# A gated linear attention with an MLP: the order of the twelve sequence pairs and the rings of the states

## The chip, the cores and the metric

The kernel runs on one core of one Trainium2 chip. Its time is the device time in microseconds (us), the median of several runs. A core has five engines that matter here: PE (matrix products), DVE and ACT (elementwise work; both can read the accumulators), POOL (elementwise work in on-chip memory only) and SP (here it issues DMAs).

## The reference

Cut to what matters, for 4 batches, 8 heads, 768 steps and a head size of 48:

```python
mag = np.sqrt(a_re * a_re + a_im * a_im)
scale = np.minimum(mag, 0.999) / (mag + 1e-06)
a_re_n, a_im_n = (a_re * scale, a_im * scale)
for t in range(S):
    S_re, S_im = ar * S_re - ai * S_im + kv[t], ar * S_im + ai * S_re
    y[t] = q[t] @ S_re
x = y, with heads side by side                # (4, 768, 384)
xn = (x - mean) / sqrt(var + 1e-6) * g_ln
out = x + relu(xn @ w_ch1) @ w_ch2            # 384 -> 1536 -> 384
```

A complex state per head is turned and shrunk at each step by a complex gate, and gains the outer product of k and v. The output of each step goes through a layer norm and an MLP with a residual.

## The kernel before, in words

Each batch is a sequence of 768 steps. It is cut into 6 chunks of 128 steps, and two chunks make a pair: 3 pairs per sequence, 12 pairs `P` in all, 24 chunks `n`. Within a chunk the recurrence is written as a small masked attention: magnitudes and phases of the gates are summed along time, keys and queries are scaled by them, and the state is carried from chunk to chunk.

For one pair the steps are these, by the names of the order table:

- `are`, `aim`, `k`, `q`, `vf`: loads, issued by SP (L400, L448, L452).
- `ln`, `iv`, `r`, `r2`, `u`, `l`, `lc`, `th`: the gates' log magnitude and angle (L455 to L492).
- `dec` on PE (L484) sums log magnitudes; `e` and `en` (L488) are its exponentials. `ph` on PE (L499, L503) sums angles, starting from the carry `car` that the pair before it in the same sequence has left (L513, L516); `sin`, `abs` or `qt`, `cos` follow.
- `ke`, `qe`, then `ks`, `qs` (all recorded at L292): keys and queries times magnitude, then times cosine and sine. Index 0 and 1 at the end are two halves.
- For each chunk: `kT`, `qT` on PE (L598) and `ksT`, `qsT` turn them, or a DMA does; `am` (L621) is the product, `atm` (L292) its masked copy; `gm` (L645) is the new part of the state and `G` the state; `gs` is a sum on the way to it, `dps` and `decc` bring the decay of a whole pair; `y` (L682, L685) is the output of the chunk.
- `bn`, `x`, `xr`, `xtr`, `xT`, `rstd`: layer norm and the turned input of the MLP.
- `mm1` (L752, six groups of six products per pair), `relu` (L764 on ACT, L766 on DVE), `mm2` (L776, three groups of four per chunk), `oa` and `ot` (scale and residual), `st` (the store).

The MLP weights come by two DMAs from POOL's queue, `wl.0` into `w1b` (L365) and `wl.1` into `w2b` (L367). `wc.J.E` (L381) then scales a block of w1b by the layer norm's gain. Before w1b is there, PE also runs `warm` products (L806, L810) whose results nobody reads.

Nothing decides the order at run time. A table `PLAN` lists every step with its engine and its accumulator bank, and each engine runs its own steps in the order of the table:

```python
vf.0.1:S th.0.0:A r2.0.0:V warm.w0:P0 ... wl.0:G@qs.0.0.0 qT.0:P2 q.2.1:S v.0:V
```

The letter is the engine (P, A, V, G for POOL, S), the digit behind it the bank. `@qs.0.0.0` makes a step on POOL wait for that DVE step too. Tiles live in rings of a fixed number of buffers (`RINGS`); a step that writes slot `i` waits until all users of `i` minus the ring's length are done. Pairs are numbered sequence by sequence (`b, pp = divmod(P, PB)`): pairs 0, 1, 2 are sequence 0, pairs 3, 4, 5 sequence 1, and so on. So the state `G` and the carry `car` pass from a pair to the next number, and rings of four and two hold them. Pair 0 is worked in two halves of the heads (`PARTS`).

Of the kernel before, what the change touches and what calls it, by code (L numbers as in the profile page):

```python
# [52 lines left out]
warm.10:P4 dec.1.0:P4 en.0.0:A7 uthc:V vf.0.0:S e.0.0:A7 r.2.0:V e.1.0:A4 warm.11:P1 warm.12:P1 dps.0:P7 are.3.0:S
r2.2.0:V en.1.0:A4 ke.0.0.0:V u.2.0:A gln:S ke.0.1.0:V qe.0.0.0:V aim.3.0:S qe.1.0.1:V qe.1.0.0:V k.1.0:S l.2.0:V
tab.trig.3:A sin.0.0:A6 sin.0.1:A0 warm.w30:P1 warm.w31:P1 warm.w32:P1 warm.w33:P1 warm.13:P1 warm.14:P1@en.1.0
warm.w34:P1 warm.w35:P1 warm.w36:P1 warm.w37:P1 warm.15:P1 warm.16:P1@qe.0.0.0 warm.w38:P1 warm.w39:P1 warm.w40:P1
warm.17:P1 warm.18:P1 warm.19:P1 warm.20:P1 qt.0.0:P6 qs.0.0.1:V sin.1.0:A2 qt.0.1:P0 ks.0.0.1:V vf.1.1:S lc.2.0:V
cos.0.0:A6 ks.0.1.1:V warm.21:P1 warm.22:P1 qt.1.0:P2 qs.1.0.1:V cos.0.1:A0 vf.1.0:S dps.1:P5 qs.0.1.1:V cos.1.0:A2
dec.2.0:P0 ks.0.1.0:V k.2.1:S ks.0.0.0:V decc.0:A7 qs.0.1.0:V kT.0:P6 decc.1:A5 qs.0.0.0:V th.2.0:A qs.1.0.0:V
wl.0:G@qs.0.0.0 qT.0:P2 q.2.1:S v.0:V qT.1:P3 ksT.0:A6 qsT.0:V2 qT.2:P4 ke.1.0.0:G@v.0 k.2.0:S kT.1:P5 qsT.1:A3  # L60
qsT.2:V4 am.0:P6 ke.1.0.1:G@v.0 ksT.1:V5 gm.0:P4 atm.0:V6 ks.1.0.1:G warm.23:P2 warm.24:P2 am.1:P2 qT.3:P5 tab.log.4:A
ln.3.0:A atm.1:V2 y.0:P6 ks.1.0.0:G G.0:A4 e.2.0:A0 warm.w41:P7 warm.25:P7 warm.26:P7 warm.27:P7 gm.1:P4 bn.0:V6
ph.2.0:P2 iv.3.0:A qsT.3:V5 one:G kT.2:P7 x.0:A6 G.1:V4 r.3.0:G en.2.0:A0 ksT.2:V7 warm.28:P5 xtr.0:P6 kT.3:P4 xT.0:V6
am.2:P0 ksT.3:V4 y.1:P5 v.1:G atm.2:V0 am.3:P6 tab.trig.5:A th.3.0:A xr.0:G gm.2:P4 bn.1:V5 ngl:G sin.2.0:A2 r2.3.0:G
ph.3.0:P0 atm.3:V6 x.1:A5 q.2.0:S car.3.0:A0 y.2:P5 G.2:V4 sin.3.0:A0 xtr.1:P7 qt.2.0:P2 are.4.0:S wc.1.1:V gm.3:P4
xT.1:A7 wc.1.0:V qt.3.0:P0 wc.1.2:V cos.2.0:A2 wl.1:G@xT.1 vf.2.0:S wc.0.0:V mm1.0.1.0:P6 wc.0.1:V cos.3.0:A0 bn.2:V5
y.3:P3 aim.4.0:S mm1.0.1.1:P6 wc.0.2:V x.2:A5 wc.2.1:V wc.2.2:V mm1.0.0.1:P0 wc.2.0:V relu.0.1:A6 bn.3:V3
qe.2.0.1:G@wc.2.0 xtr.2:P2 mm1.0.0.0:P0 xT.2:V2 x.3:V3 ke.2.0.1:G@wc.2.0 mm1.0.2.1:P6 gs.3:V4 xtr.3:P2 mm1.0.2.0:P6
rstd.1:G xT.3:V2 tab.log.6:A u.3.0:A ke.2.0.0:V mm1.1.0.1:P2 relu.0.0:A0 l.3.0:V mm1.1.1.0:P4 relu.0.2:A6 mm1.1.1.1:P4
ks.2.0.0:V lc.3.0:V mm1.1.2.1:P0 ks.2.0.1:V relu.1.1:A4 qe.2.0.0:V dec.3.0:P6 rstd.0:A qs.2.0.0:V mm1.1.0.0:P2  # L70
en.3.0:A6 qs.2.0.1:V kT.5:P4 vf.2.1:S e.3.0:A6 qT.4:P5 mm1.1.2.0:P0 ksT.5:A4 qsT.4:V5 qT.5:P6 are.5.0:S G.3:V
relu.1.2:A0 kT.4:P5 qsT.5:V6 mm2.0.0:P4 are.6.0:S ksT.4:V5 ln.4.0:A am.5:P6 mm2.0.1:P4 iv.4.0:A atm.5:V6 aim.5.0:S
mm2.0.2:P4 relu.1.0:A2 am.4:P0 r.4.0:V q.3.0:S mm2.1.0:P5 atm.4:V0 r2.4.0:A v.2:G@r.4.0 mm2.1.1:P5 q.3.1:S mm2.1.2:P5
xr.2:G@r.4.0 u.4.0:A ot.0:V4 mm2.2.0:P6 ln.5.0:A l.4.0:V st.0:S gm.4:P2 mm2.2.1:P6 iv.5.0:A G.4:V2 y.4:P0 lc.4.0:V
ln.6.0:A mm2.2.2:P6 xr.3:V k.3.0:S bn.4:V0 xr.1:G@xr.3 dec.4.0:P2 iv.6.0:A r.5.0:G@xr.3 k.3.1:S x.4:V0 y.5:P1 e.4.0:A2
dps.3:P4 bn.5:V1 xtr.4:P0 vf.3.1:S mm2.3.0:P7 oa.2:A6 xT.4:V0 en.4.0:A2 vf.3.0:S x.5:V1 mm2.3.1:P7 qe.3.0.0:G ot.1:V5
r2.5.0:A xtr.5:P0 k.4.1:S mm2.3.2:P7 rstd.2:G xT.5:V0 qe.3.0.1:V mm1.2.0.0:P0 u.5.0:A aim.6.0:S qs.3.0.0:V
mm1.2.0.1:P0 qs.3.0.1:V q.4.1:S mm1.2.2.1:P2 ke.3.0.0:V ot.3:V7 mm1.2.2.0:P2 k.4.0:S tab.trig.7:A th.4.0:A ke.3.0.1:V
qT.6:P5 relu.2.2:A2 ks.3.0.0:V ph.4.0:P6 q.4.0:S decc.3:V4 ks.3.0.1:V relu.2.0:A0 mm1.2.1.0:P2 l.5.0:V k.5.0:S kT.7:P4
abs.4.0:A6 qsT.6:V5 v.3:G@l.5.0 dps.4:P1 car.4.0:A6 kT.6:P0 vf.4.0:S ksT.7:V4 sin.4.0:A6 r.6.0:G@l.5.0 qT.7:P5  # L80
ksT.6:V0 mm1.2.1.1:P2 are.8.0:S decc.4:A1 qsT.7:V5 th.5.0:A am.6:P6 st.1:S gm.6:P4 relu.2.1:A2 ot.2:G ph.5.0:P0
atm.6:V6 are.7.0:S th.6.0:A ke.4.0.0:G am.7:P2 G.6:V4 y.6:P5 sin.5.0:A0 mm2.5.0:P6 atm.7:V2 ke.4.0.1:G vf.4.1:S
cos.4.0:A mm2.5.1:P6 qe.4.0.1:G bn.6:V5 mm2.5.2:P6 abs.5.0:A0 q.5.0:S ks.4.0.1:V y.7:P2 cos.5.0:A q.5.1:S lc.5.0:V
gm.7:P4 mm2.4.0:P7 ks.4.0.0:V x.6:A5 bn.7:V2 mm2.4.1:P7 xr.5:G@ks.4.0.0 r2.6.0:A aim.7.0:S G.7:V4 qe.4.0.0:G@ks.4.0.0
mm2.4.2:P7 x.7:V2 k.7.0:S dec.5.0:P0 qs.4.0.0:V xtr.6:P2 qs.4.0.1:V xtr.7:P3 st.2:S kT.9:P4 tab.log.8:A e.5.0:A0
xT.6:V2 v.4:G@qs.4.0.1 qT.8:P5 xT.7:V3 en.5.0:A0 ksT.9:V4 mm1.3.1.0:P2 ksT.8:S xr.4:V ln.7.0:A qT.9:P4 qsT.8:V5
qe.5.0.0:G@xr.4 mm1.3.1.1:P2 u.6.0:A qsT.9:V4 aim.8.0:S mm1.3.2.0:P0 relu.3.1:A2 l.6.0:V am.9:P4 st.3:S mm1.3.2.1:P0
iv.7.0:A k.5.1:S lc.6.0:V atm.9:V4 mm1.3.0.0:P2 qe.5.0.1:G@lc.6.0 ln.8.0:A mm1.3.0.1:P2 relu.3.2:A0 r.7.0:G@lc.6.0
ot.4:V7 dec.6.0:P4 vf.5.1:S ot.5:V6 relu.3.0:A2 gm.8:P7 ph.6.0:P0 G.8:V7 rstd.3:G vf.6.1:S en.6.0:A4 qs.5.0.1:V
am.8:P2 r2.7.0:V st.4:S e.6.0:A4 mm2.6.0:P6 qs.5.0.0:V iv.8.0:A mm2.6.1:P6 atm.8:V2 k.6.0:S xr.7:G@qs.5.0.0 mm2.6.2:P6  # L90
u.7.0:A xr.6:G@qs.5.0.0 vf.5.0:S abs.6.0:V0 r.8.0:G@qs.5.0.0 y.9:P4 y.8:P2 k.6.1:S bn.9:V4 mm2.7.0:P3 q.7.1:S bn.8:V2
gm.9:P7 tab.trig.9:A sin.6.0:A0 mm2.7.1:P3 ke.5.0.1:G gs.9:V7 are.9.0:S x.9:A4 mm2.7.2:P3 ot.6:V6 ke.5.0.0:G th.7.0:A
qT.11:P4 x.8:V2 st.6:S dps.6:P5 G.9:G cos.6.0:A car.6.0:V0 qT.10:P2 q.6.0:S qsT.11:V4 xtr.8:P6 ke.6.0.0:G xtr.9:P7
ph.7.0:P0 xT.8:A6 xT.9:V7 th.8.0:A qsT.10:V2 q.6.1:S mm1.4.1.1:P6 l.7.0:V decc.6:A5 car.7.0:A0 mm1.4.0.1:P4 abs.7.0:A0
ks.5.0.0:V mm1.4.0.0:P4 r2.8.0:V aim.9.0:S sin.7.0:A0 ks.5.0.1:V mm1.4.1.0:P6 relu.4.0:A4 lc.7.0:V kT.10:P1 ot.7:V3
q.7.0:S ke.6.0.1:G@lc.7.0 kT.11:P2 relu.4.1:A6 ksT.10:V1 k.7.1:S mm1.4.2.0:P4 ksT.11:V2 st.5:S am.10:P0 ks.6.0.1:V
am.11:P6 atm.10:V0 dec.7.0:P2 v.5:G@ks.6.0.1 tab.log.10:A rstd.4:A mm1.4.2.1:P4 ln.9.0:A vf.6.0:S xr.8:G@ks.6.0.1
# [749 lines left out]
```

## Time and profile before

| what | value |
|---|---|
| median of 3 runs | 188.05 us (187.25 to 188.61) |
| the profiled execution | 187.51 us, span 185.6 us |
| PE busy | 177.0 us, 95% of the span |
| DVE, ACT, POOL busy | 157.7, 154.6, 99.8 us |
| DMA issues by SP, share of the 16 DMA engines | 81.4% |
| moved by DMA | 35.34 MB, mean 190 GB/s |

The span runs from the first to the last instruction of the program; the device time has 1.9 us more around it. Busy time of an engine is the time in which at least one of its instructions ran. Products on PE overlap one another, so their mean duration (273 ns for one of mm1) is longer than the distance from one to the next.

### The profile page before, as it was taken

To read this page: it belongs to the slowest core of one execution; us is meant where nothing else is said; L and a number is where in the kernel's file an instruction comes from. 1 tells how busy PE (TensorE), PEld (TensorE's weight loads), DVE (VectorE), ACT (ScalarE), POOL (GpSimd) and SP (SyncE) were. 2 spreads that over 40 slices of the span, in tenths; PEclk is the share of its full clock that TensorE was granted. 3 is DMA by queue.
4 is the path that set the end of the run, shared out by engine and by line. 5 is a ranking of instruction groups with operands and counts; after the bars stand their busy time and mean duration, and the time that the engine had idled before them with its cause. 6 is when DMAs were issued, how large, how long until landed. Compare 5 with 4: busy or idle time off the path is not lost.

```text
span 185.6 us, 5131 instructions
## 1 busy us (share of the span) xinstructions
PE 177.0 (95%) x2029; PEld 139.0 (75%) x2029; DVE 157.7 (85%) x302; ACT 154.6 (83%) x218; POOL 99.8 (54%) x128
## 2 busy tenths in 40 slices
...
GB/s 154 309 229 206 246 199 191 206 143 189 262 187 213 226 228 230 212 273 181 222 238 151 168 150 241 190 227 200 183 159 139 246 147 202 163 193 73 70 82 87
DMA packets 128440, 35.34 MB, mean 190 GB/s; under 512 B 124448, under 2 KB 127648, under 8 KB 128416
## 3 DMA queue, kind: packets, MB, share of 16 engines
q1 hardware_dynamic: 127616, 32.65, 81.4%
...
HBM read 28.31 MB, written 4.72 MB: 178 GB/s over the span
## 4 chain that ended last, share of the span: by engine, by line
PE 59%; ACT 14%; DMA 10%; DVE 10%; issue 3%; SPq 2%; DVEq 0%
PE banks L752 22%; PE banks L776 19%; DMA w1b<-in_moe_w_ch_dram 7%; PE banks L598 4%; PE banks L621 4%; ACT L815 3%; PE banks L484 2%; DMA are<-in_a_re_dram 2%; DMA k<-in_k_dram 2%; ACT are L457 2%; PE banks L682 2%; DVE l L473 1%; ACT h L764 1%; PE banks L685 1%; ACT w L455 1%
## 5 line engine op out<-in xcount | busy, mean ns | idle before, releaser
L752 PE MATMUL banks<-xT,w1b 128*128 128x256 bf16 x432 | 52.7, 273 | 0.2
L776 PE MATMUL banks<-w2b,h 128*128 128x384 bf16 (+2 forms) x300 | 52.5, 319 | 0.0
L752 PEld LDWEIGHTS <-w1b 128*128 128x128 bf16 x432 | 45.8, 114 | 1.7 <-DVE w1b L381 0.4
L764 ACT ACTIVATE h<-banks 128x1024 bf16<-128x1024 f32 x33 | 32.8, 1022 | 8.3 <-PE banks L752 8.1
L776 PEld LDWEIGHTS <-h 128*128 128x128 bf16 x300 | 26.9, 97 | 14.1
L292 DVE TENSOR_TENSOR atm<-banks,mask 128x1024 bf16<-128x1024 f32 x24 | 28.9, 1218 | 1.9 <-PE banks L621 1.6
L815 ACT ACT_TABLE_LOAD x15 | 19.2, 1283 | 1.0 <-PEq L831 0.8
L292 POOL TENSOR_TENSOR ke<-k,en 128x384 bf16<-128x384 f32 x14 | 12.7, 916 | 8.3 <-DVE l L476 5.6
L292 POOL TENSOR_TENSOR qe<-q,e 128x384 bf16<-128x384 f32 x15 | 13.7, 916 | 6.1 <-DVE w1b L381 1.9
L292 POOL TENSOR_TENSOR ks<-ke,trig 128x768 bf16<-128x768 bf16 x7 | 11.4, 1643 | 6.4 <-PE banks L752 4.2
L621 PE MATMUL banks<-qsT,ksT 128*128 128x128 bf16 x192 | 14.6, 219 | 0.1
L410 POOL TENSOR_SCALAR v<-vf 128x768 bf16<-128x768 f32 x7 | 5.8, 831 | 16.0 <-DVE r L292 8.9
L810 PE MATMUL banks<-u_e 128*128 128x512 f16 x42 | 11.7, 418 | 2.2 <-POOL u_e L320 2.2
L292 POOL TENSOR_TENSOR r<-aim,are 128x768 f16<-128x768 f32 x7 | 12.7, 1817 | 1.9 <-ACT x L699 1.5
L709 POOL TENSOR_SCALAR xr<-x,mv 128x384 f32<-128x384 bf16 x16 | 9.3, 586 | 8.1 <-PE banks L752 3.3
L621 PEld LDWEIGHTS <-ksT 128*128 128x128 bf16 x192 | 12.0, 98 | 1.8 <-DVE ksT L289 0.5
L692 DVE BATCH_NORM_STATS2 stats<-banks 128x6 f32<-128x384 f32 x24 | 13.4, 556 | 0.1
L682 PE MATMUL banks<-v,atm 128*128 128x48 bf16 x192 | 12.1, 183 | 0.3 <-ACT x L699 0.2
L473 DVE SCALAR_TENSOR_TENSOR l<-r,w 128x768 f16<-128x768 f16 (+1 forms) x13 | 11.5, 892 | 0.9 <-ACT r L469 0.7
L791 DVE SCALAR_TENSOR_TENSOR ot<-banks,rstd,xr 128x384 f32<-128x384 f32 (+2 forms) x18 | 10.5, 590 | 2.0 <-PE banks L776 1.6
L455 ACT ACTIVATE w<-are 128x768 f32<-128x768 f32 (+1 forms) x13 | 10.2, 790 | 2.3 <-DMA are<-in_a_re_dram 2.3
L682 PEld LDWEIGHTS <-atm 128*128 128x128 bf16 x192 | 11.0, 96 | 1.2 <-DVE atm L292 0.2
...
## 6 DMA issues: line engine op xcount, KB each, us to landing
...
```

The lines of the kernel that those rows point to most:

```text
L292: {"DVE": nc.vector, "POOL": nc.gpsimd}[eng(name)].tensor_tensor(**kw)
L455: add(f"ln.{X}", lambda S_=S_: act(out=S_("w"), in_=S_("are"), func=AF.Ln), needs=[f"are.{X}"], uses=[("are", P), ("w", P)])
L473: nc.vector.scalar_tensor_tensor(out=S_("l"), in0=S_("r2"), scalar=0.5, in1=S_("w"), op0=ALU.mult, op1=ALU.add)
L621: nc.tensor.matmul(ps[:, h], lhsT=T("ksT", n)[:, h], rhs=T("qsT", n)[:, h], start=True, stop=True)
L682: nc.tensor.matmul(ps[:, h], lhsT=T("atm", n)[:, h], rhs=T("v", P)[:, c, h], start=True, stop=nfirst)
L692: nc.vector.bn_stats(out=T("stats", n), in_=bank(f"y.{n}")[:, 0:DM])
L752: nc.tensor.matmul(ps[:, jj], lhsT=w1b[:, dc, ts(gi, JG * C)].rearrange("k (p j) -> k j p", j=JG)[:, jj], rhs=T("xT", P)[:, dc].rearrange( ...
L764: act(out=dst, in_=src, func=AF.Relu)
L776: nc.tensor.matmul(bank(f"o.{N}")[:, ws], lhsT=T("h", P)[:, j, ts(c, C)], rhs=w2b[:, j, ws], start=(j == 0), stop=(j == NJ - 1))
L791: nc.vector.scalar_tensor_tensor(out=o, in0=bank(f"o.{N}")[:, ws], scalar=T("rstd", P)[:, ds(c, 1)], in1=xs, op0=ALU.mult, op1=ALU.add)
L810: g.add(f"warm.w{i}", lambda i=i: nc.tensor.matmul(bank(f"warm.w{i}"), lhsT=u_e[:, 0, 0], rhs=u_e.rearrange("p c j t -> p (c j t)"), start ...
L815: g.add(f"tab.{nm}.{i}", lambda tab=tab: nc.scalar.preload_act_table_set(tab))
```

## The change

Pairs are numbered the other way: first the first pairs of all four sequences (0 to 3), then the middle ones (4 to 7), then the last ones (8 to 11). The pair before pair `P` in its sequence is now `P - 4` and not `P - 1`. The state at the end of a pair therefore lives through four pairs: `G` is kept by pair, in a ring of 5, and the state in the middle of a pair moves to a ring of its own, `Gh`, of 2. The phase carry's ring grows from 2 to 4. All of this changes only which buffer a step names and which step it waits for; every step computes what it did. The order table is a new one throughout: steps stand in another order, some are given to another engine, and two warm-up products are wide that were narrow.

```diff
 RINGS = {...
-         "ks": 3, "qs": 3, "ksT": 4, "qsT": 4, "atm": 3, "G": 4, "x": 10, "stats": 4,
-         "mv": 5, "rstd": 5, "xT": 3, "h": 2, "ot": 3, "car": 2, "gt": 2, "xr": 3}
+         "ks": 3, "qs": 3, "ksT": 4, "qsT": 4, "atm": 3, "G": 5, "Gh": 2, "x": 10, "stats": 4,
+         "mv": 5, "rstd": 5, "xT": 3, "h": 2, "ot": 3, "car": 4, "gt": 2, "xr": 3}
...
 def pair_ops(P):
-    b, pp = divmod(P, PB)
+    pp, b = divmod(P, B)
+    was = P - B
+    back = was * R + R - 1
...
-                + ([] if first else [f"car.{P - 1}.{x}" for x in range(PARTS.get(P - 1, 1))]),
+                + ([] if first else [f"car.{was}.{x}" for x in range(PARTS.get(was, 1))]),
...
-                        act(out=T("car", P + 1)[96:C, fs], ...
+                        act(out=T("car", P + B)[96:C, fs], ...
...
                 elif c == 0:
-                        f"G.{n}", out=T("G", n), ..., in1=T("G", n - 1), op=ALU.add),
-                        needs=[f"gm.{n}", f"G.{n - 1}"], uses=[("G", n), ("G", n - 1)],
+                        f"G.{n}", out=T("Gh", P), ..., in1=T("G", was), op=ALU.add),
+                        needs=[f"gm.{n}", f"G.{back}"], uses=[("Gh", P), ("G", was)],
...
-                        nc.tensor.matmul(ps[:, h], lhsT=T("qsT", n)[:, h], rhs=T("G", n - 1)[:, h],
+                        nc.tensor.matmul(ps[:, h], lhsT=T("qsT", n)[:, h], rhs=(T("Gh", P) if c else T("G", was))[:, h],
...
-for i in range(29):   # warm.i, 256 columns
+for i in range(27):
-for i in range(42):   # warm.wi, 512 columns
+for i in range(44):
```

In the order tables, around the trigger of w1b (before, then after):

```diff
-qs.0.0.1:V ... ks.0.0.1:V ... lc.2.0:V ... ks.0.1.1:V ... qs.1.0.1:V ... qs.0.1.1:V ... ks.0.1.0:V ... ks.0.0.0:V
-... qs.0.1.0:V ... qs.0.0.0:V th.2.0:A qs.1.0.0:V wl.0:G@qs.0.0.0
+lc.2.0:V ... decc.1:V2 ... qs.0.1.1:V ks.0.1.1:V cos.0.0:A3 qs.0.0.1:V warm.17:P1 warm.18:P1 qt.1.0:P6 wl.0:G@qs.0.0.1
```

and around the first mm1:

```diff
-wc.1.1:V gm.3:P4 xT.1:A7 wc.1.0:V qt.3.0:P0 wc.1.2:V cos.2.0:A2 wl.1:G@xT.1 vf.2.0:S wc.0.0:V mm1.0.1.0:P6
+wc.2.2:V warm.25:P1 xtr.0:P0 atm.2:V2 car.3.0:A4 xtr.1:P1 wc.2.1:A ... wc.2.0:A xT.0:V0 are.4.0:S xT.1:V1 gm.2:P2
+cos.3.0:A4 wc.1.2:V y.2:P3 mm1.0.2.1:P0 wc.0.0:V wc.0.1:V wl.1:G@wc.0.0
```

More of the change, by code (lines that the diff above doesn't have):

```diff
@@ L53 @@
[L53 to L97, printed above, removed]
@@ L138 @@
[L138 to L141 removed]
+ue:G are.1.0:S are.0.0:S are.0.1:S pad.qs.1:G car0.0:G aim.1.0:S ident:G pad.ks.0:G mask:G aim.0.0:S tab.log.0:A
+ln.1.0:A pick:G aim.0.1:S iv.1.0:A one:G car0.1:G aim.2.0:S pad.qs.0:G ln.0.0:A car0.3:G ln.0.1:A zdec:G qrow:G
@@ new lines @@
+qs.2.0.0:V tab.log.6:A u.3.0:A ks.2.0.1:V mm1.1.2.1:P4 relu.1.1:A6 qs.2.0.1:V mm1.1.2.0:P4 ks.2.0.0:V relu.0.1:A0
+qT.5:P3 pad.ks.2:G@ks.2.0.0 mm1.1.0.1:P6 xr.0:G@ks.2.0.0 qsT.5:V3 relu.1.2:A4 kT.4:P0 l.3.0:V kT.5:P1 ksT.4:A0
+vf.2.1:S mm1.1.0.0:P6 G.3:V2 lc.3.0:V qT.4:P3 ksT.5:V1 uec:G@lc.3.0 dec.3.0:P4 are.5.0:S ln.4.0:A qsT.4:V3 am.5:P0
+uthc:V rstd.1:A mm2.0.0:P2 atm.5:V0 iv.4.0:A xr.1:G@uthc q.3.1:S mm2.0.1:P2 relu.1.0:A6 mm2.0.2:P2 r.4.0:V q.3.0:S
+e.3.0:A4 am.4:P0 r2.4.0:V mm2.2.0:P3 aim.5.0:S atm.4:V0 u.4.0:A v.2:G@r2.4.0 mm2.2.1:P3 en.3.0:A4 mm2.2.2:P3 rstd.0:G
@@ new lines @@
+l.5.0:V aim.6.0:S kT.7:P4 tab.trig.7:A th.5.0:A decc.3:V7 mm1.2.2.0:P0 ke.4.0.0:G@l.5.0 q.4.1:S ksT.7:V4 relu.2.0:A2
+ph.5.0:P6 relu.2.2:V0 xr.3:G@l.5.0 st.2:S th.4.0:A ke.4.0.1:G kT.6:P4 ot.3:V5 am.7:P2 sin.5.0:A6 are.7.0:S xr.4:G
+ksT.6:V4 ph.4.0:P0 abs.5.0:A6 v.3:G atm.7:V2 mm1.2.1.0:P4 car.5.0:A6 are.8.0:S car.4.0:A0 am.6:P6 lc.5.0:V sin.4.0:A0
+st.1:S gm.6:P2 r.6.0:G@lc.5.0 mm1.2.1.1:P4 atm.6:V6 G.6:A2 aim.7.0:S abs.4.0:A0 mm2.5.0:P3 relu.2.1:V4 y.7:P6
+cos.4.0:A qe.4.0.0:G y.6:P0 k.5.1:S mm2.4.0:P1 th.6.0:A bn.7:V6 qe.4.0.1:G gm.7:P2 mm2.5.1:P3 cos.5.0:A x.7:V6 q.5.1:S
@@ new lines @@
+ks.4.0.0:G mm2.5.2:P3 bn.6:V0 r2.6.0:A vf.4.1:S dps.4:P4 x.6:V0 xtr.7:P5 mm2.4.1:P1 decc.4:V4 xr.5:G vf.4.0:S xT.7:V5
+xtr.6:P0 mm2.4.2:P1 G.7:V2 qs.4.0.1:G tab.log.8:A ln.7.0:A xT.6:V0 dec.5.0:P6 k.5.0:S ot.4:V1 u.6.0:A mm1.3.1.0:P4
+ot.5:V3 st.4:S e.5.0:A6 qs.4.0.0:V mm1.3.1.1:P4 l.6.0:V iv.7.0:A qT.9:P0 q.5.0:S mm1.3.2.0:P2 ks.4.0.1:V en.5.0:A6
+k.6.0:S lc.6.0:V mm1.3.2.1:P2 qsT.9:V0 relu.3.1:A4 qe.5.0.1:G@lc.6.0 dec.6.0:P6 st.3:S relu.3.2:V2 v.4:A
+r.7.0:G@lc.6.0 kT.9:P0 vf.5.0:S qT.8:P1 e.6.0:A6 ksT.9:V0 mm1.3.0.1:P2 q.6.1:S qsT.8:V1 en.6.0:A6 gm.8:P0 xr.6:G
@@ new lines @@
+am.9:P4 G.8:V0 vf.6.1:S r2.7.0:A mm1.3.0.0:P2 ke.5.0.1:G atm.9:V4 k.6.1:S kT.8:P1 u.7.0:A xr.7:G gm.9:P0 aim.8.0:S
+ph.6.0:P6 ksT.8:V1 ke.5.0.0:G relu.3.0:A2 gs.9:V0 aim.9.0:S am.8:P4 rstd.3:G ln.8.0:A l.7.0:V mm2.6.0:P1 abs.6.0:A6
+ks.5.0.0:V mm2.6.1:P1 vf.5.1:S ks.5.0.1:V iv.8.0:A mm2.6.2:P1 k.8.0:S atm.8:V4 qe.5.0.0:G@ks.5.0.1 y.9:P2 mm2.7.0:P0
+qs.5.0.0:V vf.6.0:S y.8:P3 bn.9:V2 qs.5.0.1:G@qs.5.0.0 tab.trig.9:A th.7.0:A mm2.7.1:P0 bn.8:V3 mm2.7.2:P0 sin.6.0:A6
+x.8:V3 ph.7.0:P4 car.6.0:A6 q.6.0:S r.8.0:G cos.6.0:A x.9:V2 xtr.8:P3 ot.7:V0 are.9.0:S qT.11:P2 abs.7.0:A4 dps.5:P6
@@ new lines @@
+qsT.11:V2 sin.7.0:A4 qe.6.0.1:G xtr.9:P0 qT.10:P7 k.7.1:S decc.5:V6 kT.11:P2 car.7.0:A4 xT.8:V3 ke.6.0.1:G xT.9:V0
+th.8.0:A kT.10:P6 st.5:S ksT.11:V2 mm1.4.0.1:P4 qsT.10:A7 lc.7.0:V ksT.10:V6 am.11:P2 G.9:G@lc.7.0 mm1.4.0.0:P4 v.5:A
+atm.11:V2 ke.6.0.0:G@lc.7.0 am.10:P6 relu.4.0:A4 vf.7.1:S dps.6:P0 ot.6:V1 qe.6.0.0:G mm1.4.1.1:P2 k.8.1:S atm.10:V6
+mm1.4.1.0:P2 xr.9:G st.6:S dec.7.0:P4 r2.8.0:V tab.log.10:A ln.9.0:A q.7.0:S mm1.4.2.0:P6 relu.4.1:V2
+qs.6.0.0:G@r2.8.0 e.7.0:A4 mm1.4.2.1:P6 are.10.0:S decc.6:V0 en.7.0:A4 gm.10:P1 y.10:P2 relu.4.2:V6 ks.6.0.1:G
```

164 lines of the change are left out of this document (91 added, 73 removed).

## The prediction

> **What bounds the kernel now.** I began with the page's busy times, because they say which engines can be the limit at all.
>
> ```profile
> PE 177.0 (95%) x2029; PEld 139.0 (75%) x2029; DVE 157.7 (85%) x302; ACT 154.6 (83%) x218; POOL 99.8 (54%) x128
> ```
>
> Three engines stand over 80%, so a share over the whole span decides nothing. Next comes the view by stretches of time (per engine: busy us and count of instructions, then the granted clock, the DMA share and GB/s).
>
> ```profile
> 35.00:40.00 5.00, 4.72 (x69) 3.51 (x68) 4.51 (x13) 4.43 (x8) 1.50 (x2) 1.00 0.69 157
> ...
> 110.00:120.00 10.00, 9.89 (x131) 8.06 (x130) 9.27 (x17) 9.68 (x15) 7.86 (x8) 1.00 1.07 209
> ...
> 180.00:185.60 5.60, 2.00 (x23) 1.61 (x21) 1.45 (x3) 0.00 (x0) 0.00 (x0) 1.00 0.21 72
> ...
> 40.00:180.00 140.00, 139.82 (x1658) 114.98 (x1657) 125.02 (x234) 118.69 (x163) 80.21 (x88) 1.00 0.90 189
> 40.00:120.00 80.00, 79.85 (x945) 65.37 (x944) 76.15 (x143) 78.17 (x108) 46.73 (x50) 1.00 0.98 207
> ```
>
> Between 40 and 180 us PE is busy for 139.82 of 140 us, at a granted clock of 1.00. In the stretch 40 to 120 ACT idles for 80 - 78.17 = 1.83 us and DVE for 80 - 76.15 = 3.85 us, so PE has two close followers. After 120 us both have room. The chain of waits shows what sets the start and the end of PE's full stretch (start, length, what).
>
> ```profile
> 23.86 0.67 DVE qs L292 x2
> 24.53 12.18 DMA w1b<-in_moe_w_ch_dram
> ...
> 36.81 0.20 DVE w1b L381
> ...
> 37.08 0.36 DVE w1b L381
> ...
> 37.48 0.89 PE banks L752 x6
> ...
> 81.75 0.56 DVE G L292
> ...
> 117.49 0.84 PE banks L752 x6
> ...
> 143.22 0.20 PE banks L645 x8
> 143.43 0.45 PE banks L621 x8
> ...
> 149.56 1.95 PE banks L776 x12
> ...
> 174.12 3.96 PE banks L752 x36
> 178.07 3.94 PE banks L776 x36
> ...
> 182.11 0.35 DVE ot L791
> ```
>
> The load of w1b is triggered at 24.53 us, behind a DVE product, and lands 12.18 us later; the first mm1 starts at 37.48. From there PE runs until about 182.0, and the last eviction and store end the span at 185.6. So the time is: start of the first mm1, plus PE's remaining work, plus whatever PE loses on the way, plus 3.5 us of tail. A new order cannot make the remaining work smaller; it can move the start, and it can add or remove losses.
>
> Does PE wait for the states, which are what the change is about? In the view of waits (engine and what it was about to make, what released it: total us, times, longest):
>
> ```profile
> DVE G L292 <- PE banks L645: 3.2, 5, 1.3
> ...
> DVE xT L289 <- PE banks L719: 2.8, 3, 1.3
> ...
> PE banks L503 <- ACT th L492: 0.9, 1, 0.9
> ```
>
> PE's wait at L503 is for the arctangent of the first pair. No PE wait on a state or on a phase carry is listed. The G waits are DVE's, for PE's own product. Nothing visible on PE is there to be freed.
>
> **The change part by part, and the sum.** *Amount of work.* Counting the two order tables, PE has the same groups of every kind, except two warm-up products of 256 columns fewer and two of 512 more, all ahead of the first mm1, where PE waits for w1b in any case: nothing. Transposes, table loads and DMAs are equal in number. So is the PE work left at the first mm1: ahead of it gm.3 has gone and dps.2 has come, eight short products each.
>
> *Longer rings.* Five tiles G plus two Gh for four G, four carries for two: two more memsets on POOL, of which POOL's 54% leaves room. Nothing. If a carry were late, a ph would wait; in the new order each carry is needed four pairs later, not one.
>
> *Front, trigger of w1b.* It now waits behind qs.0.0.1 and not behind qs.0.0.0. Counting DVE's queue up to the trigger, five half products, one whole product and uthc move behind it; one ke and a decc (two small copies) come ahead of it.
>
> ```profile
> L292 DVE TENSOR_TENSOR qs<-qe,trig 128x768 bf16<-128x768 bf16 x18 | 9.6, 552 | 0.2
> ...
> L292 DVE TENSOR_TENSOR ke<-k,en 128x384 bf16<-128x384 f32 x10 | 5.4, 549 | 0.0
> ...
> L292 DVE TENSOR_TENSOR qs<-qe,trig 128x384 bf16<-128x384 bf16 x4 | 1.3, 354 | 0.0
> ...
> L333 DVE TENSOR_SCALAR u_thc<-u_ec 128x256 f16<-128x256 f16 x1 | 0.2, 217 | 0.0
> ...
> L289 DVE COPY dec<-banks 48x8 f32<-48x8 f32 x6 | 0.9, 153 | 0.0
> ```
>
> That is 5 x 0.354 + 0.552 + 0.217 - 0.549 - 2 x 0.153 = 1.68 us. Neighbours overlap, as the timeline shows for two half products and a whole one just before the trigger:
>
> ```profile
> 23.59 1.09 DVE L292 TENSOR_TENSOR qs<-qe,trig 128x384 bf16<-128x384 bf16 x3
> ```
>
> They took 1.09 us where 2 x 0.354 + 0.552 = 1.26, so 0.08 us per neighbour, four instructions net, and I take 1.4: trigger at 23.1, landing at 23.1 + 12.2 = 35.3 instead of 36.7. But the first mm1 does not follow the landing as closely as before. Before, wc.1.1, wc.1.0 and wc.1.2 stood between landing and mm1: 37.48 - 36.71 = 0.77 us. Now the first scaled block, wc.2.2, stands in DVE's queue ahead of atm.2, xT.0 and xT.1, and mm1 needs both xT:
>
> ```profile
> L292 DVE TENSOR_TENSOR atm<-banks,mask 128x1024 bf16<-128x1024 f32 x24 | 28.9, 1218 | 1.9 <-PE banks L621 1.6 <-ACT h L764 0.3
> ...
> L289 DVE COPY xT<-banks 128x384 bf16<-128x384 bf16 x14 | 4.8, 349 | 2.8 <-PE banks L719 2.8
> ...
> L381 DVE TENSOR_SCALAR w1b<-w1b,ngl 128x512 bf16<-128x512 bf16 x9 | 2.7, 365 | 0.5 <-DMA w1b<-in_moe_w_ch_dram 0.5
> ```
>
> 0.365 + 1.218 + 2 x 0.349 = 2.28 us, less overlaps some 2.0, plus 0.1 to start: first mm1 at 35.3 + 1.9 = 37.2 or so. **Front: -0.3 us.** Bounds: -1.4 if DVE's part hides, +0.5 if w1b shares the DMA engines worse and lands at its old time less half a microsecond.
>
> *Front, w2b.* Its trigger is put behind wc.0.0, which comes after xT.1 and one more block, near 37.8. The old one, from the timeline, with the first mm2, and the landing time from the view of the tile w2b:
>
> ```profile
> 37.46 0.83 POOL L367 DMA_DIRECT2D w2b<-in_moe_w_ch_dram  x1 [1.79 <-ACT xT L287]
> ...
> 48.81 0.82 PE L776 MATMUL banks<-w2b,h 128*128 128x384 bf16 x4
> ...
> DMA to landing us min/median/max: 11.3/11.3/11.3
> ```
>
> It landed at 37.46 + 11.3 = 48.8, just as PE got there. In the new order it lands near 49.1, and PE, which now has am.5 and gm.3 ahead of it too (0.45 + 0.20 us by the spacing of such groups in the chain), gets there at about the same time. Nothing, or up to +0.5.
>
> *Middle.* Here engines change places. Up to the first mm1 of pair 7, DVE's queue gains five ReLUs, four xT, two r, two r2, four decc and single others, and loses four wc, four xr, three G, two abs, two ke, two qs and single others: by the rows' means +14.1 and -10.5, net +3.6 us. The ReLUs alone:
>
> ```profile
> L766 DVE TENSOR_SCALAR h<-banks 128x1024 bf16<-128x1024 f32 x3 | 3.6, 1214 | 3.3 <-PE banks L752 3.3
> ...
> L764 ACT ACTIVATE h<-banks 128x1024 bf16<-128x1024 f32 x33 | 32.8, 1022 | 8.3 <-PE banks L752 8.1
> ...
> L408 ACT CAST v<-vf 128x768 bf16<-128x768 f32 x3 | 2.5, 843 | 1.0 <-DMA vf<-in_v_dram 1.0
> ...
> L292 POOL TENSOR_TENSOR ke<-k,en 128x384 bf16<-128x384 f32 x14 | 12.7, 916 | 8.3 <-DVE l L476 5.6
> ```
>
> 5 x 1.214 = 6.1 us to DVE. PE's queue up to the same point grows by 1.5 us (one more am, four more short groups, one more transpose). DVE therefore runs 3.6 - 1.5 = 2.1 us later against PE. ACT sheds 5 x 1.022 = 5.1 us, takes four casts of v (3.4) and smaller pieces, net +0.4, so it runs 1.1 us earlier against PE: the engine with the smaller reserve (1.83 us) is relieved, the one with the larger (3.85) is loaded. POOL gains 7.6 us, much of it ke at 0.916, within its 80 - 46.73 = 33 us of idle time. If DVE's idle time shrinks by what is added, PE loses nothing; if DVE keeps all its idle time, PE loses 2.1. I take +0.5, near the lower end, because PE's busy time shows no place where DVE held it in the old order. **Middle: +0.5 us (0 to +2.1).**
>
> *End.* Both tables close with pair 11's mm1 and mm2 unbroken, then one eviction and a store: 3.96 + 3.94 us and the 3.5 behind it. Nothing.
>
> **Sum:** the profiled execution took 187.51 us (span 185.6, 1.9 around it), 0.54 under the median of 188.05. 187.51 - 0.3 + 0.5 = 187.7 us.
>
> **The rivals.** *Slower: DVE becomes the bound between 40 and 120 us.* Of its 3.85 us of reserve 2.1 are spent; 1.75 us remain for all waits of eight tens of microseconds, and PE waits for DVE from there on. For it: DVE idled about 0.73 us in the stretch 110 to 120, and its waits for gm and xtr (3.2 and 2.8 us) do not vanish with the order. At 0.73 per ten, DVE idles 5.8 us in that stretch, PE waits 5.8 - 1.75 = 4.1, and the time is 187.51 - 0.3 + 4.1 = 191.3. It passes 1% once DVE keeps about what it idles now. Against it: DVE idles most where it is ahead. The Trainium skill (SBUF — State Buffer, section "SBUF: two separate sides") says that DVE and GpSimd share a port pair as an exclusive lock, so that a DVE operation with two SBUF inputs waits out a GpSimd one that reads SBUF. By that rule POOL's added 7.6 us could cost DVE up to as much, and the time would be 187.2 + 7.6 = 194.8 at most. I count that inside this rival: the view of waits lists no DVE wait on POOL after the constants are made, and the order table has such turns written in by hand.
>
> *Faster: the full PE hides gaps that the new order closes.* Busy PE need not be PE at its pace. The pace itself is in the chain: 36 products of mm1 in 3.96 us (110 ns each) and 12 of mm2 in 1.95 (163 ns). From 81.75 to 117.49 the chain runs over other engines while PE counts as busy. Summing all groups by such spacings gives some 143 us for the 144.5 from first mm1 to last, so 1.4 us at most are hidden. With a front of -1.1 the time is 187.51 - 1.4 - 1.1 = 185.0. Against it: all of both terms must come. The Trainium skill (Perfetto Trace Analysis, section "Identifying the Most-Contended Engine") warns that matmul busy time says little and that weight-load busy time should be read. By that, 114.98 of 140 would leave 25 us to win; the spacings disagree.
>
> *The change does nothing it says:* state chains leave no PE wait before, so freeing them is worth nothing. That is my forecast's ground, not a case apart.
>
> **How the numbers follow.** 1% of 188.05, about what a measurement of this kernel can tell from no change, is 1.9 us: faster means under 186.2, slower over 189.9. Forecast (186.2 to 189.9, its own bounds are 187.5 - 1.4 = 186.1 and 187.5 + 0.5 + 0.5 + 2.1 = 190.6, so it is cut at these) 0.48; DVE bound 0.35; hidden gaps closed 0.17. The range runs from just above the faster case to just past the slower one: 185.4 to 191.8.
>
> **What would show it.** Right: w1b's trigger near 23.1, first mm1 near 37.2, PE idle under 1 us from 40 to 180, DVE busier than 76.15 and ACT less than 78.17 in 40 to 120. Slower case: PE waits on atm, xT or a DVE ReLU between 60 and 120, DVE idle over 4 us there. Wrong altogether: a first mm1 more than 1.5 us off, PE waiting for a load or for POOL, or a longer tail.

## The result, and the profile after

| | before | after |
|---|---|---|
| device time, median of 22 runs each | 187.57 us | 188.61 us |
| lowest of them | 187.02 us | 188.16 us |
| span of the profiled execution | 185.6 us | 186.7 us |

The ratio is 1.0052, with a 95% interval of 1.0031 to 1.0073: the change costs about 1 us. The ratios here and below are worked out from all the executions of both kernels, without the few that took over 1.5% more than the quickest of their kernel, so they can differ from the quotient of the two medians, by up to 0.2%. The forecast was 187.7 us. Its terms add 0.2 us to the profiled execution (187.51), and against the median then shown (188.05) it is a gain of 0.2%. Measured is a loss of 0.5%.

The rows that answer to those of before. First the page's busy times:

```profile
PE 178.6 (96%) x2029; PEld 138.7 (74%) x2029; DVE 156.8 (84%) x299; ACT 156.9 (84%) x220; POOL 103.1 (55%) x131
```

Then the view by stretches of time (start:end and length, then busy us of PE, PEld, DVE, ACT, POOL, granted clock, DMA share, GB/s):

```profile
40.00:120.00 80.00, 79.63 (x957) 64.50 (x956) 76.30 (x144) 77.38 (x104) 54.72 (x62) 1.00 1.00 210
120.00:180.00 60.00, 59.17 (x698) 49.03 (x696) 47.75 (x84) 42.68 (x63) 28.80 (x30) 1.00 0.83 167
40.00:180.00 140.00, 138.80 (x1652) 113.53 (x1651) 124.05 (x227) 120.06 (x166) 83.51 (x92) 1.00 0.93 192
```

PE's idle time between 40 and 180 us went from 140 - 139.82 = 0.18 us to 140 - 138.80 = 1.20 us. Most of it, 0.83 us, lies behind 120 us, in the stretch that I had expected to be unbroken. DVE (76.15 before, 76.30 now) and ACT (78.17, now 77.38) hardly moved. The chain of waits says what PE idled for (start, length, what):

```profile
36.40 0.72 ACT w1b L379
37.16 2.15 PE banks L754 x18
...
101.95 5.92 DMA ksT<-ks
107.92 0.62 PE banks L623 x8
...
144.41 4.59 DMA ksT<-ks
149.04 0.62 PE banks L623 x8
...
165.35 4.57 DMA ksT<-ks
169.97 0.62 PE banks L623 x8
...
175.72 3.93 PE banks L754 x36
179.65 3.94 PE banks L778 x36
```

Three transfers of the same kind are now links of the chain. The old chain had no such link; behind the load of w1b it held one load of k. Each is a turn: SP's DMA transposes a finished tile ksT (keys of one chunk, 128 x 1024) instead of PE. The tiles are ksT.12, ksT.19 and ksT.23, and L623 is am, the product that reads them. By the distance of the matmul groups, PE lost 0.45 us ahead of am.12, 0.42 ahead of am.19 and 0.71 ahead of am.23, 1.58 us together. The page's group of am says the same (at the right: idle us before, and what ended it):

```profile
L623 PE MATMUL banks<-qsT,ksT 128*128 128x128 bf16 x192 | 14.7, 219 | 1.1 <-DMA ksT<-ks 1.1
L623 PEld LDWEIGHTS <-ksT 128*128 128x128 bf16 x192 | 11.9, 97 | 4.0 <-DMA ksT<-ks 1.9
```

The sum of the difference: first mm1 0.3 us sooner (37.16 for 37.48), last matmul group 1.6 us later (ending at 179.65 + 3.94 = 183.6 for 182.0), tail 0.5 us shorter (186.7 - 183.6 = 3.1 for 3.6), so 1.1 us of span.

### The profile page after: what moved, and what is told of

It reads as the page before. It is cut to its first block, busy times and chain, and to the rows that moved or that the text cites. A ratio compares the mean times of both kernels' runs of the same rounds, so it can differ in the third digit from the quotient of the medians.

```text
span 186.7 us, 5149 instructions
## 1 busy us (share of the span) xinstructions
PE 178.6 (96%) x2029; PEld 138.7 (74%) x2029; DVE 156.8 (84%) x299; ACT 156.9 (84%) x220; POOL 103.1 (55%) x131
## 4 chain that ended last, share of the span: by engine, by line
PE 63%; DMA 11%; DVE 10%; ACT 7%; issue 3%; POOL 2%; SPq 2%; POOLq 0%; ACTq 0%; DVEq 0%
PE banks L754 19%; PE banks L778 19%; DMA ksT<-ks 8%; PE banks L600 7%; PE banks L623 5%; DMA are<-in_a_re_dram 2%; PE banks L505 2%; PE banks L684 2%; DVE atm L292 2%; DVE l L475 2%; PE banks L486 2%; DVE r L292 2%; PE banks L687 2%; PE banks L721 1%; ACT L817 1%
## 5 line engine op out<-in xcount | busy, mean ns | idle before, releaser
L778 PEld LDWEIGHTS <-h 128*128 128x128 bf16 x300 | 27.3, 98 | 14.4 <-ACT h L766 0.2
L766 ACT ACTIVATE h<-banks 128x1024 bf16<-128x1024 f32 x27 | 27.4, 1022 | 11.3 <-PE banks L754 9.7
L292 POOL TENSOR_TENSOR qe<-q,e 128x384 bf16<-128x384 f32 x14 | 13.0, 935 | 11.4 <-DVE l L478 3.0
L292 POOL TENSOR_TENSOR ke<-k,en 128x384 bf16<-128x384 f32 x18 | 16.4, 920 | 2.5 <-DVE qs L292 1.4
L623 PE MATMUL banks<-qsT,ksT 128*128 128x128 bf16 x192 | 14.7, 219 | 1.1 <-DMA ksT<-ks 1.1
L812 PE MATMUL banks<-u_e 128*128 128x512 f16 x44 | 13.1, 436 | 2.6 <-POOL u_e L320 2.2
L791 POOL TENSOR_TENSOR ot<-ot,xr 128x384 f32<-128x384 f32 x7 | 7.0, 1001 | 14.7 <-ACT ot L783 12.1
L623 PEld LDWEIGHTS <-ksT 128*128 128x128 bf16 x192 | 11.9, 97 | 4.0 <-DMA ksT<-ks 1.9
L711 POOL TENSOR_SCALAR xr<-x,mv 128x384 f32<-128x384 bf16 x17 | 10.0, 591 | 5.8 <-DVE ks L292 2.6
L292 POOL TENSOR_TENSOR r<-aim,are 128x768 f16<-128x768 f32 x6 | 10.9, 1817 | 3.1 <-DVE qs L292 2.2
L768 DVE TENSOR_SCALAR h<-banks 128x1024 bf16<-128x1024 f32 x9 | 11.0, 1220 | 1.8 <-PE banks L754 1.6
L292 DVE TENSOR_TENSOR r<-aim,are 128x768 f16<-128x768 f32 (+1 forms) x7 | 5.8, 836 | 7.9 <-ACT are L459 7.9
L292 POOL TENSOR_TENSOR qs<-qe,trig 128x768 bf16<-128x768 bf16 x6 | 9.9, 1646 | 3.8 <-DVE qs L292 1.6
```

The lines of the kernel that those rows point to most:

```text
L292: {"DVE": nc.vector, "POOL": nc.gpsimd}[eng(name)].tensor_tensor(**kw)
L623: nc.tensor.matmul(ps[:, h], lhsT=T("ksT", n)[:, h], rhs=T("qsT", n)[:, h], start=True, stop=True)
L766: act(out=dst, in_=src, func=AF.Relu)
L768: nc.vector.tensor_scalar(out=dst, in0=src, scalar1=0.0, scalar2=None, op0=ALU.max)
L778: nc.tensor.matmul(bank(f"o.{N}")[:, ws], lhsT=T("h", P)[:, j, ts(c, C)], rhs=w2b[:, j, ws], start=(j == 0), stop=(j == NJ - 1))
L812: g.add(f"warm.w{i}", lambda i=i: nc.tensor.matmul(bank(f"warm.w{i}"), lhsT=u_e[:, 0, 0], rhs=u_e.rearrange("p c j t -> p (c j t)"), start ...
```

## The experiments

In the order table, `name:S` is an instruction of SP's queue, which issues in the order of the table. A tile is called late when PE has come to its product before it has landed.

### Are the late turns the loss?

My theory was that the three turns simply stand too late in SP's queue: ksT.12 behind a load with 29 us of slack, ksT.19 behind qsT.19, ksT.23 behind xT.20 and qsT.23, although its input was ready 7.6 us before its issue. The rival was that other limits stand right behind them. Four kernels tell these apart, two with the turns moved in the changed kernel, one with a turn moved in the kernel before, one with the front's edit alone.

**Turns earlier**, in the changed kernel:

```diff
-q.7.0:S are.10.0:S k.9.1:S q.7.1:S ksT.12:S ... vf.7.0:S
+q.7.0:S q.7.1:S are.10.0:S ksT.12:S ... vf.7.0:S k.9.1:S
-xT.16:S qsT.18:S qsT.19:S ksT.19:S
+qsT.18:S xT.16:S ksT.19:S qsT.19:S
-xT.21:S ksT.22:S qsT.22:S xT.20:S qsT.23:S ksT.23:S
+ksT.23:S xT.21:S ksT.22:S qsT.22:S xT.20:S qsT.23:S
```

> Only SP's order differs from the changed kernel: the turns of ksT.12, ksT.19 and ksT.23 by DMA stand earlier in SP's queue (q.7.1 and k.9.1 out of the way of ksT.12, ksT.19 ahead of qsT.19, ksT.23 ahead of xT.21). Theory (late turns): in the changed kernel am.12, am.19 and am.23 wait 0.45, 0.42 and 0.71 us for the landing of these tiles, 1.58 us together; here ksT.23 lands near 161 instead of 169.9, ksT.19 near 145.5 instead of 149.0 and ksT.12 near 106 instead of 107.9, the three waits fall under 0.15 us each, and the last PE end comes 1.2 to 1.6 us sooner (183.6 to about 182.2): ratio to the kernel before 0.995 to 0.999. Rival (another limit stands right behind, VectorE, ScalarE or GpSimd late in the new order): the waits move to other inputs of the same or the next matmuls, the PE end stays within 0.4 us of 183.6, ratio 1.003 to 1.006.

Measured: 187.55 us against 187.48, ratio 0.999 (0.996 to 1.002). ksT.12 landed at 106.03, ksT.19 at 145.12, ksT.23 at 160.23, and no am waits for a turn. The last PE end is 181.9. The view by stretches of this kernel:

```profile
40.00:180.00 140.00, 139.75 (x1660) 114.44 (x1658) 123.76 (x227) 120.12 (x166) 83.92 (x92) 1.00 0.91 189
```

PE's idle time is back at 0.25 us. So the loss of the change is these turns, to within 0.3%; no other limit stands right behind them.

**A turn later**, in the kernel before:

```diff
-qsT.23:S ksT.23:S st.16:S st.17:S st.18:S
+qsT.23:S st.16:S st.17:S st.18:S ksT.23:S
```

> The kernel before, with one transfer put later in SP's queue: the turn of ksT.23 stands behind the stores st.16, st.17 and st.18. Its issue goes from 163.80 to about 165.4 (three stores of 0.4 to 0.6 us), its landing from 166.96 to about 168.6; am.23 began at 167.98, so its slack of 1.0 us is used up. Theory (a late turn costs the end its lateness): am.23 waits 0.5 to 0.7 us and the whole run is longer by that, ratio 1.002 to 1.004. Rival (a wait of this size is made up behind it, since the last 14 us have other slack): ratio within 0.001 of 1.

Measured: 189.73 us, ratio 1.0136 (1.0084 to 1.0189), some three times what I expected, also without the two of its six executions with a clock of 0.991 and less (191.22 and 191.79; the other four 189.43 to 189.75). The issue ended 1.8 us later than in the kernel before (166.93 for 165.13), but the landing came 3.1 us later (170.06 for 166.96), and PE waited 2.4 us. The direction fits the theory, the size does not: something held this transfer for 1.3 us more. The timeline of SP, and the DMA view from 165 to 171 us (40 slices of 0.15 us, busy tenths of the 16 DMA engines, then GB/s), show what:

```profile
165.64 1.29 SPq L604 DMA_TRANSPOSE ksT<-ks  x1
...
DMA  9999999999898999999999001000070000000000
GB/s 189 349 396 369 369 359 399 369 359 358 236 276 255 203 212 207 323 213 189 196 92 9 0 2 9 9 10 9 14 124 0 0 0 0 0 0 0 0 0 0
...
q8 instruction: 1, 0.02, 1.1%
```

From 168.15 to 169.35 us the DMA engines move 0 to 14 GB/s, with the turn in flight. Then the rest of it passes in one slice, and 0.6 us later it has landed. In the same window a single packet of 16 KB, of kind "instruction", was on queue q8; it started at 167.5.

**A turn later**, in the changed kernel:

```diff
-xT.20:S qsT.23:S ksT.23:S st.17:S ... st.16:S
+xT.20:S st.17:S st.16:S qsT.23:S ksT.23:S
```

> The changed kernel with the stores st.16 and st.17 put ahead of the turns of qsT.23 and ksT.23 in SP's queue, 0.4 to 0.55 us of issue each. Theory: ksT.23 lands about 1.0 us later (near 170.9), the wait of am.23 grows from 0.71 to about 1.7 us, and the PE end goes from 183.6 to about 184.5: ratio to the kernel before about 1.010. Rival (other waits of the last stretch overlap with this one): less than half of that reaches the end, ratio 1.005 to 1.007.

Measured: 189.22 us, ratio 1.0078 (1.0052 to 1.0104), between the two. am.23 waited 1.62 us. But ksT.23, issued 0.45 us later, landed only 0.2 us later (170.15), again right behind a stop of the DMA engines with an instruction packet at 167.4. The place in the queue is half of the story only.

**The front alone**, in the kernel before:

```diff
-... qs.0.0.1:V ... qs.0.0.0:V ... wl.0:G@qs.0.0.0
+... qs.0.0.1:V wl.0:G@qs.0.0.1 ... qs.0.0.0:V
```

> The kernel before with one edit of the change alone: w1b's trigger hangs on qs.0.0.1 instead of qs.0.0.0, which there ends at 21.60 instead of 24.21, so the trigger goes from 24.5 to about 21.8. Landing: by the 12.2 us of the kernel before near 34.0, by the 9.2 us of the changed kernel near 31.0. The first product of the MLP (mm1.0.1.0, 37.48) then waits for xT.1 on ScalarE (37.15) and the phases' qt.3.0 instead of wc.1.0 (37.42), so it comes 0 to 0.3 us sooner. Theory (front worth a few tenths): ratio 0.998 to 1.000. Rival (loads pushed behind w1b come late and hold the middle): slower, ratio over 1.002.

Measured: 187.71 us, ratio 0.9996 (0.9965 to 1.0027). With the earlier trigger (21.9) w1b lands 9.5 us behind it. Whether the edit gains or loses 0.3 us can't be told at this width. The profile doesn't say it either: the first mm1 came at 38.54 there, but in this execution, the longest of its ten, PE was granted half its clock from 23.9 us on for 3.4 us (the page's row, 40 slices of the span, tenths of the full clock):

```profile
PEclk9999969999999999999999999999999999999999
```

### What is in the way of the turns?

The page of the changed kernel counts the packets of q8:

```profile
q8 instruction: 16, 0.26, 0.6%
```

They start 8.4 to 14.4 us apart, and between the first (21.4 us) and the last (181.9) PE starts 3820 matmuls and weight loads, 3820 / 15 = 255 for each in the mean. I read them as PE's own program, fetched in pieces of 16 KB; that they move with the number of PE's instructions is shown below. In the changed kernel they start at 104.8, 146.7 and 167.5 us, among other places, and each of the three late tiles lands behind one of these. The DMA view of the changed kernel from 167 to 171 us (slices of 0.1 us):

```profile
DMA  9999999999900000000000079896000000000000
GB/s 220 187 202 202 215 379 205 166 208 244 54 0 0 0 3 8 8 8 10 10 10 8 13 261 445 338 445 231 0 0 0 0 0 0 0 0 0 0 0 0
...
q8 instruction: 1, 0.02, 1.6%
```

From 168.1 to 169.3 nearly nothing moves; ksT.23 lands at 169.92. So a second theory: a turn that is in flight when an instruction packet comes is held for about a microsecond, and the new order puts three turns under packets. The rival: the stops belong to the traffic or to that execution.

**The same kernel again**, to see whether the places recur.

> The changed kernel once more, unedited, to see what in its profile comes back. In all six profiles so far a packet of 16 KB of TensorE's instructions (queue q8, one about every 256 TensorE instructions, 10 us apart) starts near 104, 146 and 167 us, and the DMA engines then stand nearly still for 1 to 1.3 us if turns are in flight; in the changed kernel the three late tiles land right behind these stops (107.87, 149.00, 169.92). Theory (instruction packets): packets within 1 us of 104.8, 146.7 and 167.5 again, am.19 and am.23 waiting 0.3 to 0.8 us each again. Rival (the waits were chance of that execution): they stand at other matmuls. Ratio 1.003 to 1.007 by both.

Measured: 188.26 us, ratio 1.0031 (1.0007 to 1.0055). Packets at 103.7, 145.9 and 167.4; am.19 waited 0.32 us, am.23 1.12, am.12 nothing. Two of the three waits recur. ksT.12 again took 3.4 us from the end of its issue to its landing, but was issued 1.0 us sooner, so am.12 had no wait. (Not all six profiles have the packets near these places: in the one of the front alone they start at 107.2, 149.0 and 169.4.)

**Packets moved, nothing else.** The packets follow the count of PE's instructions, so they can be moved by the warm-up ahead of the real work: a matmul of 512 columns becomes `parts` matmuls of 512 / `parts`, equal in columns, with 2 (`parts` - 1) more instructions.

```diff
+        parts = 4 if i < 30 else 1
-        g.add(f"warm.w{i}", lambda i=i: nc.tensor.matmul(
-            bank(f"warm.w{i}"), ..., rhs=u_e...
+        g.add(f"warm.w{i}", lambda i=i, parts=parts: [nc.tensor.matmul(
+            bank(f"warm.w{i}")[:, ts(x, 512 // parts)], ..., rhs=u_e...[:, ts(x, 512 // parts)],
+            ...) for x in range(parts)], ...
```

The changed kernel with 180 more (30 matmuls in four):

> The changed kernel; each of the first 30 wide warm-up matmuls of 512 columns is issued as four of 128 columns: equal time, 180 more TensorE instructions (with their weight loads) before 15 us, and nothing else is changed. TensorE reaches every 256th instruction 180 earlier, so the instruction packets come 7.35 us earlier, which puts the next ones near 107.8, 149.1, 160.2 and 173.8, that is 2.5 to 3 us behind the places where they held ksT.12, ksT.19 and ksT.23. Theory (a packet holds the turn that is in flight): these tiles land near 106.1, 147.7 and 168.7, the waits of am.12, am.19 and am.23 fall under 0.2 us each (1.58 us in the changed kernel), the last PE end comes 1.0 to 1.6 us sooner, ratio 0.996 to 1.000. Rival (the order of SP's queue alone makes them late, the stops go with the traffic or the time): the same three waits, ratio 1.003 to 1.007.

Measured: 187.11 us against 187.56, ratio 0.9969 (0.9949 to 0.999); the unedited changed kernel took 188.26 in the same round. The first mm1 came at 36.82 us, in the unedited repeat at 36.90. The packets came at 107.8, 149.0, 158.7 and 169.4; ksT.12, ksT.19 and ksT.23 landed at 105.24, 146.84 and 167.63. The stretch and the group of am in this kernel:

```profile
40.00:180.00 140.00, 139.87 (x1662) 114.61 (x1660) 123.82 (x227) 120.16 (x166) 83.81 (x92) 1.00 0.91 186
...
L623 PE MATMUL banks<-qsT,ksT 128*128 128x128 bf16 x192 | 14.6, 219 | 0.0
```

No am waits, though SP's queue is in the order of the changed kernel to the last transfer. ksT.23 was issued at 164.45, and from 165 us to its landing nothing stops (slices of 0.1 us, from 165):

```profile
164.45 1.33 SPq L605 DMA_TRANSPOSE ksT<-ks  x1
...
DMA  9999996699999999999999999300000000000000
```

The zeros at the end stand behind its landing, with nothing left to move. This kernel has the lowest median of all.

The changed kernel with 72 more (36 matmuls in two):

> The changed kernel; each of the first 36 wide warm-up matmuls is issued as two of 256 columns: equal time, 72 more TensorE instructions, so the packets come 2.9 us earlier, near 101.9, 143.8 and 164.6. Theory: am.12, am.19 and am.23 are free (under 0.2 us each); instead qsT.18 (landing 144.87, am.18 at 145.73) and xT.20 (landing 165.06, its matmul at 165.57) are held, to about 146.2 and 167.0, so 0.3 to 0.6 us at am.18 and 0.8 to 1.4 us at mm1.10.0.1; ratio 1.002 to 1.007. Rival: the same three waits as in the changed kernel, ratio 1.003 to 1.007; the places tell them apart, not the time.

Measured: 187.99 us, ratio 1.0018 (0.9989 to 1.0047). Packets at 101.5, 144.0 and 164.9. am.12, am.19 and am.23 are free, and am.18 waits 0.94 us for qsT.18, which lands at 146.0. The chain of waits now has this tile:

```profile
141.09 4.93 DMA qsT<-qs
```

The place is as expected, the price higher (0.3 to 0.6 expected); the time alone can't be told from no change. The second place did not come: xT.20 landed at 165.0, just ahead of the stop at 166.0 to 167.0.

The kernel before with 36 more (18 matmuls in two):

> The kernel before; each of the first 18 wide warm-up matmuls is issued as two of 256 columns: 36 more TensorE instructions, so the packets come 1.5 us earlier: near 105.0, 145.8 and 166.3 instead of 106.5, 147.3 and 167.8. In the kernel before, ksT.23 landed at 166.96, 0.8 us ahead of the packet. Theory: the packet now meets ksT.23 in flight, it lands near 168.7, am.23 (167.98) waits 0.5 to 0.9 us, ratio 1.002 to 1.005. Rival (the packets hold nothing): ratio within 0.0015 of 1.

Measured: 188.82 us, ratio 1.0061 (1.0038 to 1.0084). am.23 waited 0.77 us for ksT.23, and am.20 another 0.47 for ksT.20, issued under the packet at 156.9, which I had not expected. Their sum, 1.24 us, is the size of the measured 188.82 - 187.56 = 1.26, but that is in part luck: the profiled execution was the longest of its twelve (190.26), and PE waited in it for w2b too, which took 12.6 us to land (from the view of waits: total us, times, longest):

```profile
PE banks L776 <- DMA w2b<-in_moe_w_ch_dram: 1.6, 1, 1.6
```

What the median execution waited for is not shown. But none of the twelve took less than 188.28 us, where the kernel before has a lowest time of 186.98. So the kernel before can be made as slow as the changed one without touching its order.

The changed kernel with 252 more (42 in four), nearly one whole packet:

> The changed kernel; each of the first 42 wide warm-up matmuls is issued as four of 128 columns: 252 more TensorE instructions, which is nearly one whole packet of 256. The packets come one place earlier in number and so at nearly the same times as without the edit, near 104, 146 and 167. Theory (their phase against the turns decides): the waits of am.19 and am.23 are back (0.3 to 1.2 us each, 0.8 to 1.6 us together), last PE end near 183.2, ratio 1.002 to 1.006. Rival (splitting the warm-up matmuls is itself what gained 1.15 us in the kernel with 180 more): as fast as that one or faster, ratio 0.995 to 0.999.

Measured: 187.85 us against 187.23, ratio 1.0032 (1.002 to 1.0043). The page counts 17 packets instead of 16, those near 104.3 and 147.2 are back at their places, and so are waits: am.19 0.89 us, am.12 0.29. am.23 stayed free here, its packet came at 169.7. PE also waited 0.62 us ahead of mm2.0.0 in this execution, the longest of its six, for w2b, which has nothing to do with the turns. The ratios to the kernel before, 1.0032 here and 0.9969 with 180 more, lie clear of each other: the gain there was the place of the packets, and not the split.

To see that the 180 were not a lucky number, 168 (28 in four):

> The changed kernel with 168 more TensorE instructions (28 wide warm-up matmuls as four each) instead of 180: packets 0.5 us later than there, near 98.3, 108.3, 118.4, 149.5, 159.2 and 169.9, still clear of ksT.12 (landing 105.2), ksT.19 (146.8) and ksT.23 (167.6). Theory (phase decides, and 0.5 us is no matter there): no wait of am.12, am.19 or am.23 over 0.2 us, ratio 0.996 to 1.000, again 0.4 to 0.8% under the unedited changed kernel. Rival (the fast result with 180 more was luck of that count): 1.002 to 1.007.

Measured: 187.21 us against 187.29, ratio 0.9984 (0.9958 to 1.001), no wait of the three.

Last, the kernel before with 180 and with 252 more:

> The kernel before with the same 180 more TensorE instructions in its warm-up: packets near 109.4, 119.3, 139.9, 151.9, 160.5 and 172 instead of 106.5, 116.8, 136.3, 147.3, 159.3 and 167.8. Of its turns, ksT.22 (landing 162.10, used at 164.23) and qsT.22 (163.03) are met near 160.5 and keep 0.2 to 1 us of slack; ksT.17, ksT.19, ksT.23 are not met. Theory (the kernel before was hit by no packet at a place where TensorE waits, so it has nothing to gain, and nothing is hit here): ratio 0.998 to 1.002, and the changed kernel without hits (0.9969) stays 0.2 to 0.6 us ahead of it, which is the order's own worth. Rival (the split gains by itself): 0.994 to 0.997.

> The kernel before with 252 more TensorE instructions in its warm-up (42 wide warm-up matmuls as four of 128 columns each), nearly one whole packet, so that its packets come at nearly their old times (106.5, 147.3, 167.8). Open is why the kernel before with 180 more came out 0.58% longer with no wait for a turn in its profile. If the split itself costs (the warm-up's clock, or TensorE late in the front): ratio 1.003 to 1.006 here too. If it is the packets' phase: no turn is met where TensorE waits, ratio 0.998 to 1.002.

Measured: 188.20 us against 187.23, ratio 1.0058 (1.0033 to 1.0084), with 180, which neither theory nor rival had; 187.70 us against 187.29, ratio 1.0001 (0.9978 to 1.0025), with 252. The second says that splitting the warm-up costs nothing by itself that this width could show. For the first, no PE wait for a turn stands in the profile; PE waited 0.51 us ahead of mm2.0.0, for w2b, and the profiled execution was the quickest of its eight (187.47). Three of the eight had a mean granted clock of 0.991, like the execution of the front's kernel above, and took 188.42 to 189.41 us. The other five have a median of 187.80, 0.3% over the kernel before, so the clock goes with about half of the excess. Where the rest was lost stays open, and a hit by packets in executions without a profile is not excluded.

## Why the prediction was wrong

**The step that failed**, under "Amount of work", is one sentence: "Transposes, table loads and DMAs are equal in number." It was true (19 turns in each kernel), and I priced them at nothing; in the profile three of them cost PE 1.58 us. What counts is where a turn stands: in SP's queue against the product that reads it, and against PE's instruction packets. The trace of before has the landing times of every turn; ksT.23 had 1.0 us of slack there (166.96 against 167.98). From the new table I worked out no issue or landing behind the front, so the three tiles without slack could not show. Of the signs named for a right forecast, the trigger, the first mm1 and the busy times of DVE and ACT came, but PE's idle time was 1.20 us and not under 1. The text named "PE waiting for a load" as a sign that it was wrong altogether; a turn is not a load from memory, but a wait of this kind came.

**Middle, +0.5 us by DVE (0 to +2.1).** The cause was wrong. PE's idle time between 40 and 180 us grew by 1.02 us, which lies in the range, but by luck: DVE's busy time in 40 to 120 grew by only 0.15 us, and PE waited for DMA. With the turns out of the way (by the queue, or by the packets) PE's idle time is 0.25 and 0.13 us. The rival that DVE becomes the bound, 191.3 us, is not seen in any run.

**Front, -0.3 us.** The size was right: 37.16 forecast as 37.2. w1b's trigger came at 23.14 (23.1 forecast). That the sum came out is luck, since two of its steps did not: w1b landed at 32.4 and not at 35.3, and the gate was not DVE's atm.2 and xT.1, which was done at 36.73, but ACT's two scaled blocks of w1b, from 35.77 to 37.10 (the row of L379 above is the later part). The gain itself is no chance of one profile: the first mm1 came at 36.82 to 37.16 in all eight profiles with the new order, and at 37.14 to 37.48 in the old order, without the one at half clock.

**w2b.** Triggered at 37.57 (37.8), landing 10.9 us later, at 48.5 (49.1); mm2.0.0 at 49.11, not held. Right for this execution; in four of the 14 profiles PE waited 0.5 to 1.7 us there.

**End, nothing.** The unbroken closing work is as forecast, 3.93 and 3.94 us. The tail of 3.5 us became 3.1; I have no experiment on that.

**Gaps closed, 185.0 us.** Not seen. In the three kernels of the new order where PE waits for no turn (turns earlier, 180 more, 168 more), the ratios are 0.9969, 0.9984 and 0.999, and only the first is clear of 1. So the order's own worth is 0.2 to 0.6 us at these ratios; that this is the front is argued from the first mm1, not shown by a run.

The Trainium skill (DMA: Bandwidth & Descriptors, section "Rules for kernel authors") says to issue a DMA early and wait for it late, so that its fixed cost overlaps. The runs agree: the kernel with ksT.23 issued 8.6 us sooner had no wait for it, with the last packets within 1 us of their old places (145.8 and 166.7 for 146.7 and 167.5). The same section says that a transpose next to ordinary DMAs needs nothing. That speaks of the data; the runs show that its time is not equal everywhere.
